# Attention with learned feature maps beside a Mish feed-forward, on one core: key weights moved to ACT's queue, with a new order of all steps

## The chip, the core and the metric

The kernel runs on one core of one Trainium2 chip. The metric is the device time of one execution in microseconds (us). Three runs of the kernel before took 149.74, 149.78 and 149.93 us, so its median is 149.78. The engines are TensorE (PE, with its weight loads PEld), VectorE (DVE), ScalarE (ACT), GpSimd (POOL) and SyncE (SP). ACT and SP also issue the DMAs; each has a queue of its own for them.

## The reference

One block of a model on 2048 tokens of width 448. A layer norm without weights feeds two branches, whose results are added to the input:

```python
xn = _layernorm(x)
# branch A: linear attention, 16 heads of width 28
q, k, v = split(xn @ wqkv)
pq, pk  = q @ w_phi, k @ w_phi                       # per head
phi_q   = concat(softmax(pq), softmax(-pq))          # 56 features per head
phi_k   = concat(softmax(pk), softmax(-pk))
kv, z   = phi_k^T @ v, sum over tokens of phi_k
o       = (phi_q @ kv) / (phi_q @ z + 1e-6)
# branch B
h   = xn @ w1 + b1                                    # 1792 wide
act = h * tanh(softplus(h))                           # Mish
out = x + o @ wo + act @ w2
```

All inputs are bf16.

## The kernel before, in words

**Tiles.** The 2048 tokens are 16 tiles of 128 (`t`), handled in 8 pairs (`u`). The width 448 is three rows of 128 and a rest of 64 rows. So that the array is full, the rest rows of the two tiles of a pair are multiplied at the same time, each in one half of the array's rows. Work for a pair is cut into parts: `E` and `O` are three matmuls over all 128 rows for the even and the odd tile; `A` and `B` are six half-row matmuls each, which run two at a time; `H` is the rest, two half-row matmuls. `E`+`O`+`H` and `A`+`B`+`H` give the same result.

**Weights.** The feature maps are folded into the projections: `W @ w_phi` is made on the core for queries (`Wpq`) and keys (`Wpk`). For the keys the weights are turned on PE in two halves (`w_tr`, L548: eight transposes each, step names `wtk0`, `wtk1`), copied out of PSUM into `Eq0`, multiplied by the block matrix `Wbd` that holds `w_phi` (`w_mm`, L572, steps `wmk0`, `wmk1`), and copied to `Wpk`. The query weights come already turned by the DMA (`lqT0` to `lqT3`, L312), their last 64 columns are doubled by DVE (`qd`, L316), and `wmq0`, `wmq1` multiply them. The first transposes of the keys (half 1) want three loads: `Wkv` rows 0 to 383 of the keys (`lkm`, L303), and the last 64 rows of keys and values twice, once for each half of the array (`lkt`, L308, called tails here). The value weights are `lvm`, L303. The load of `w_phi` (`lp`, L329, four DMAs) must follow the clearing of `Wbd` on POOL (`pwp`, L378).

**Stages.** At the start `x` is loaded in pairs of tiles or four tiles (`lx4.6`: tiles 4 and 5). DVE or ACT take mean and variance (`st`), ACT or POOL the reciprocal root (`rs`, `rp`), DVE or ACT normalize (`xn`), and PE with a copy (`xt..E`, `xt..O`, L514) or a DMA on SP (`xt..m`, L525) turn the result to `xnT`. Then come the projections: `v` (copied by ACT or DVE), `k` and `q` (each followed by two exponentials on ACT, L613 and L679), with the first parts of the feed-forward `f` (Mish on ACT, L698) in between. Key features are normalized by DVE sums and reciprocals (L621, L623) and a product on POOL or DVE (`kn`, L625); query features go through DMA transposes on SP (`e`, L687). `kv` (L643) sums over the tokens, `kvz` brings that sum through a DMA transpose into `KVZ`, `nd` (L721) gives numerators and denominators, DVE divides, `ot` (L758) turns the result, and `wo` (L861) and `gx`, `g` (L842, L827) add both branches into PSUM; DVE adds `x`, and the output is stored.

**What sets the order.** The table `ORDER` names all steps, and `run_order` calls them in that order. Each engine, and each engine's DMA queue, carries out its own part of that list strictly in order; before an instruction stand waits for what it needs from other engines. `s`, `a`, `d`, `p` at the end of a name choose the engine (SP, ACT, DVE, POOL), `b` for `wtk` means both ACT and DVE, each half of the copy. PSUM is eight banks, taken as four pairs: a projection takes the pair that was left longest ago, and PE must wait until the copy or the exponentials that read it have ended.

**The start in this order.** POOL makes zeros, the identity matrix (`pi`) and the other constants. `warm` multiplies zeros (L406), to keep PE busy before data is there. `b1` (L692) turns the bias, between 10 and 4 of these.

```python
def load_main(eng, name, dst, src):                                        # L302
    dma(eng, lambda e: e.dma_start(dst[:, 0:3, :], ...), w=[(name, 0)], tag="ld" + name)
...
r = rows_of("Wk")[:1 + 2 * h] + [("ident",)]                               # L550
```

Of the kernel before, what the change touches and what calls it, by code (L numbers as in the profile page):

```python
# [176 lines left out]


ORDER = """
zero pi ph pp0 table lx6.8a z10 lx4.6s pwp lkms lba st4d lps lkta lx2.4s st5d st6d pe st7a pp1 lvms b1 rp4a z4 xn4d xn5d pp2 rp6a pv xn6d  # L180
lx12.16s lqT3 lqT2 wtk1a xt2Ea xn7d wtk0d lqT1 xt3Ea xt2Oa xt3Od st3d wmk1a st2d wmk0a rp2p st12d lqT0 st15a st14d v2Ba lx8.12s v3Ha v2Ha
v3Aa xn3d v2Aa v3Ba rp14p qd k2H lx0.2s k2E xn2d st13d wmq0d wmq1a k2O xn15a k3E k3O q2B rp12p st8d xn12d q3A xn13d st9d xt1m ep l1ts xn14d
k3H rp8p q2H xn8d xn9d q2A q1B st10d q3B xt6m st11d xt7m st1d q1A st0d xt4m rp10p v1Bd q3H v1Hd v1Ad rp0p k1H xn1d q1H k1O k1E l1ms k6E k6O
k4E xn0d xn11d k4O xt0Ed e6 e7 xt0Od e2 e3 k6H k4H xn10d v4Bd k7A v4Ad kn1.1p v4Hd k7H kn6.0p k0B k7B k0H k0A q6B v7Ba q6H v0Aa v7Aa v7Ha
q6A xt5m v0Ba kn7.0p kn2.1d e5 e4 q4B v0Ha f0.2B q4H q4A f0.3B f0.2A kn3.1p f0.3H f0.3A kn6.1p f0.2H f0.0B kn0.1p kn7.1p v5Bd pk f0.0H f0.0A
kn2.0p v5Ad v5Hd q5A e13 q5H q0A e12 q5B v6Bd l2.2s e8 k5A l2.0a q0H kn0.0p kn4.1p los v6Ad v6Hd kn4.0p q0B kn1.0d k5H f0.12A f0.12H k5B
f1.12B kn5.1d kn5.0p kn3.0d kv6 kv7 kv0 f1.12H f1.12A e9 f1.0A f1.0H f0.12B f1.0B f0.7B kv1 kv4 kv2 f0.8H f0.7A f0.8A f0.7H f0.13H f0.8B
f0.13A f1.8B f0.13B kv5 kv3 e10 f1.8H kvz f1.10B f1.11B f1.10H e11 f1.10A f1.11H f0.10H f1.8A f1.11A f0.1H f0.10A f0.1A f1.3H f0.10B nd5
f1.3A f0.1B f1.7B f1.3B f1.7A f1.7H nd7 q7H q7A f0.6A q7B f1.1A nd6 f0.6H e0 f1.1B f0.6B f0.11B f1.6A f1.1H f1.6H f0.11A f1.6B e15 f0.11H
l2.3a e14 f1.9A f1.2B f0.4B f1.2A f1.2H ot3m nd3 e1 f1.9H f0.4A f1.9B f0.5H f0.4H f0.9B f0.5B nd0 f0.9A f1.13B f0.9H f0.5A f1.5B f1.13H nd2  # L190
f1.13A l2.1s f1.5A f1.4B f1.5H ot1m nd4 f1.4A gx3A nd1 gx2A ot2m wo3A wo3H wob nd11 f1.4H ot0m gx3B wo3B nd13 wo1H gx1A nd12 ot6m wo2A wo2H
gx0A nd9 wo0B wo2B wo1A gx2B gx1B wo1B wo0A nd8 gx6B nd15 gx6A nd10 ot4m sto3 ot5m gx4A nd14 sto1 gx0B gx4B wo6H ot7m wo5H wo0H wo6B gx5B
wo5B wo7H wo4A wo6A wo5A gx5A wo7A wo4B wo7B wo4H g14 g15 sto4 sto2 sto5 sto0 stt14 sto6 stt15
"""


# [809 lines left out]
```

## Time and profile before

| | |
|---|---|
| median of three runs | 149.78 us (149.74 to 149.93) |
| the profiled execution | 149.73 us, of which the span of the instructions is 147.9 |
| PE busy | 143.0 us, 97% of the span, 1844 matmuls |
| DVE, ACT, POOL busy | 106.6, 77.9, 28.9 us |
| chain that ended last | PE 92%, DMA 3%, ACT 2%, ACT's queue 1%, DVE 1% |
| granted TensorE clock | 1.00 |
| DMA | 17.02 MB, 115 GB/s mean |

Times in the views are from the start of the span. A matmul's duration in the views is longer than its share, since matmuls follow one another before the last has ended; what one costs in a row is the distance from start to start. Two half-row matmuls run side by side, so a row of `x28` with half rows is 14 pairs. A wait is put down to what came last; "issue" is time in which nothing is waited for.

### The profile page before, as it was taken

The page shows a single profiled execution, that of the slowest core. Times are in us where ns is not written, and L with a number is a line of the kernel's source. Part 1 is how long each engine was busy: PE and PEld are TensorE (multiplying, and loading weights), DVE is VectorE, ACT ScalarE, POOL GpSimd, SP SyncE. Part 2 cuts the span into 40 slices and gives each one's busy share as a digit, 9 for nine tenths or more (in the row PEclk, how much of TensorE's full clock was granted, in tenths as well). Part 3 has the DMA queues.
Part 4 walks back from the last instruction along what each step waited for, and adds up shares of the span by engine and source line. Part 5 has one row for each costly group of instructions (what it writes and reads, how often), then busy time and mean ns, then how long its engine had stood idle before and what let it go on. Part 6 is the DMA issues. An engine that isn't in the chain of part 4 may idle for free.

```text
span 147.9 us, 4201 instructions
## 1 busy us (share of the span) xinstructions
PE 143.0 (97%) x1844; PEld 76.3 (52%) x1844; DVE 106.6 (72%) x217; ACT 77.9 (53%) x96; POOL 28.9 (20%) x41
## 2 busy tenths in 40 slices
PE   7699999999999999999999999999999999999993
PEld 2275445555555554445444445555555555556652
DVE  0899987999999997217942889979973999433432
ACT  3699999999998966778997583030000000000000
POOL 5005333373999606000000000000000000000000
DMA  5997998998999400090069502220020040600063
GB/s 132 301 243 224 169 184 277 226 160 203 114 329 275 50 4 0 20 194 7 0 146 225 156 4 62 66 62 0 4 64 4 0 124 4 177 14 0 0 241 131
DMA packets 39125, 17.02 MB, mean 115 GB/s; under 512 B 33092, under 2 KB 38340, under 8 KB 39108
## 3 DMA queue, kind: packets, MB, share of 16 engines
q1 hardware_dynamic: 37704, 15.40, 47.4%
q10 hardware_dynamic: 1404, 1.36, 3.1%
q8 instruction: 14, 0.23, 0.7%
q14 instruction: 3, 0.02, 0.1%
HBM read 7.02 MB, written 1.84 MB: 60 GB/s over the span
## 4 chain that ended last, share of the span: by engine, by line
PE 92%; DMA 3%; ACT 2%; ACTq 1%; DVE 1%; issue 0%
PE PS L441 51%; PE PS L842 25%; PE PS L861 7%; PE PS L827 3%; DMA Wkv<-in_A_wqkv_dram 3%; PE PS L721 2%; PE PS L643 2%; ACT xnT L519 1%; ACT Eq L519 1%; PE PS L572 1%; ACTq L337 0%; PE PS L548 0%; DVE x_all L792 0%; ACTq L308 0%; ACT L357 0%; PE PS L514 0%
## 5 line engine op out<-in xcount | busy, mean ns | idle before, releaser
L441 PE MATMUL PS<-xnT,W 64*128 64x512 bf16 x392 | 45.2, 376 | 0.0
L842 PE MATMUL PS<-W,actT 64*128 64x448 bf16 x392 | 39.1, 349 | 0.0
L698 ACT ACTIVATE actT<-PS,b1T 128x1024 bf16<-128x1024 f32 x28 | 29.9, 1113 | 14.5 <-PE PS L441 14.5
L441 PEld LDWEIGHTS PS<-xnT,W 64*128 64x128 bf16 x392 | 18.8, 94 | 20.3 <-ACT actT L698 0.4
L842 PEld LDWEIGHTS PS<-W,actT 64*128 64x128 bf16 x392 | 19.0, 94 | 16.7
L625 POOL TENSOR_TENSOR actT<-actT,rSk 128x896 bf16<-128x896 bf16 x12 | 20.1, 1698 | 12.9 <-DVE rSk L623 12.9
L792 DVE TENSOR_TENSOR x_all<-PS,x_all 128x448 bf16<-128x448 f32 (+1 forms) x16 | 9.3, 616 | 16.0 <-PE PS L861 9.4
L621 DVE TENSOR_REDUCE Sk<-actT 128x32 f32<-128x896 bf16 x16 | 16.8, 1049 | 0.0
L613 ACT ACTIVATE actT<-PS 128x896 bf16<-128x896 f32 x16 | 13.8, 941 | 0.3 <-PE PS L441 0.2
L441 PE MATMUL PS<-Wkv,xnT 64*128 64x448 bf16 x112 | 12.9, 350 | 0.3 <-ACT xnT L519 0.3
L441 PE MATMUL PS<-Wpq,xnT 64*128 64x448 bf16 x112 | 13.0, 349 | 0.0
L441 PE MATMUL PS<-Wpk,xnT 64*128 64x448 bf16 (+1 forms) x82 | 12.6, 351 | 0.0
L480 DVE BATCH_NORM_STATS2 stats<-x_all 128x6 f32<-128x448 bf16 x14 | 8.5, 605 | 4.2 <-DMA x_all<-in_A_x_dram 4.2
L737 DVE COPY Sq<-PS 128x32 f32<-128x32 f32 x16 | 3.0, 186 | 11.8 <-PE PS L721 11.8
L746 DVE TENSOR_TENSOR v_all<-v_all 128x464 f32<-128x464 f32 x16 | 10.3, 642 | 0.6
L742 DVE TENSOR_TENSOR v_all<-PS,Sq 128x464 f32<-128x464 f32 x16 | 10.3, 641 | 0.5
L750 DVE TENSOR_TENSOR xn<-v_all,rden 128x448 bf16<-128x448 f32 x16 | 10.0, 625 | 0.6
L744 DVE TENSOR_TENSOR v_all<-PS,Sq 128x464 f32<-128x464 f32 x16 | 10.1, 629 | 0.0
L679 ACT ACTIVATE actT<-PS 128x896 bf16<-128x896 f32 x10 | 8.8, 946 | 0.0
L441 PEld LDWEIGHTS PS<-Wkv,xnT 64*128 64x128 bf16 x112 | 5.6, 94 | 5.4 <-PE PS L441 0.9
L441 PEld LDWEIGHTS PS<-Wpq,xnT 64*128 64x128 bf16 x112 | 5.7, 94 | 4.7 <-DVE stats L480 0.4
L441 PEld LDWEIGHTS PS<-Wpk,xnT 64*128 64x128 bf16 (+1 forms) x82 | 5.5, 95 | 5.0 <-issue 0.7
(82 smaller groups left out, 133.8 us busy)
## 6 DMA issues: line engine op xcount, KB each, us to landing
out_dram<-x_all SPq DMA_DIRECT2D x7, 224.0 KB, 2.2
W<-in_B_w_dram SPq DMA_DIRECT2D x1, 1344.0 KB, 7.5
x_all<-in_A_x_dram SPq DMA_DIRECT2D x2, 448.0 KB, 4.3
x_all<-in_A_x_dram SPq DMA_DIRECT2D x3, 224.0 KB, 3.7
Wkv<-in_A_wqkv_dram SPq DMA_DIRECT2D x2, 336.0 KB, 4.3
Wo<-in_A_wo_dram SPq DMA_DIRECT2D x2, 336.0 KB, 4.1
W<-in_B_w_dram SPq DMA_DIRECT2D x2, 224.0 KB, 3.8
W<-in_B_w_dram ACTq DMA_DIRECT2D x1, 448.0 KB, 4.1
```

Of the source, the lines that this page charges most:

```text
L441: ins = e.matmul(o, lhs(c, k), rhs(c, k), start=par in first and n == at[par][0], stop=par in last and n == at[par][-1])
L613: op("ACT", lambda e, s=s: e.activation(E_of(u)[:, s, :, :], two(b, D), ACT.Exp, scale=1.0 if s == 0 else -1.0), r=[pb(b), pb(b + 1)], w=[ ...
L621: op("DVE", lambda e: e.tensor_reduce(Sk[u][:, s, :], Eh(), AX.X, ALU.add), r=[("E", u, s)], w=[("Sk", u, s)], tag=f"Sk{u}.{s}")
L625: op(eng, lambda e: e.tensor_tensor(Eh(), Eh(), ap_on(rSk[u][:, s, 0:1], [[1, 2 * H], [0, DH]]), ALU.mult), r=[("E", u, s), ("rSk", u, s)] ...
L698: op("ACT", lambda e: e.activation(actT[:, fc, q * 1024:(q + 1) * 1024], bank(b, 2), ACT.Mish, bias=b1T[:, fc:fc + 1]), r=[("b1T",), pb(b) ...
L742: op("DVE", lambda e: e.tensor_tensor(tv(t1), num(0), sx(1), ALU.mult), r=[pb(b), pb(b + 1), ("Sq", i)], w=[("t1", i)], tag=f"ta{t}")
L744: op("DVE", lambda e: e.tensor_tensor(tv(t2), num(1), sx(0), ALU.mult), r=[pb(b), pb(b + 1), ("Sq", i)], w=[("t2", i)], tag=f"tb{t}")
L746: op("DVE", lambda e: e.tensor_tensor(t1, t1, t2, ALU.add), r=[("t1", i), ("t2", i)], w=[("t1", i)], tag=f"tc{t}")
L750: op("DVE", lambda e: e.tensor_tensor(o_sb[k][:, t % 2, :].rearrange("p (h d) -> p h d", d=DH), t1[:, :, 0:DH], ap_on(rden[i][:, 0:1], [[1 ...
L792: op("DVE", lambda e: e.tensor_tensor(x_all[:, t, 0:n], bank(b)[:, 0:n], x_all[:, t, 0:n], ALU.add), r=[pb(b), ("x", t)], w=[("out", t)], ...
L842: ins = e.matmul(bank(b)[:, 0:D], actT[lo:hi, fc, tok(2 * u + par)], W2[lo:hi, fc, 0:D], start=first and fc == 0, stop=last and fc == FC - 1)
L861: ins = e.matmul(bank(b)[:, 0:w], oT_of(u)[lo:hi, cc * P:(cc + 1) * P], Wo[lo:hi, cc, 0:w], start=first and n == at[par][0], stop=last and ...
```

## The change

Only the table `ORDER` is changed; every step's code is as it was. Its first lines, before and after:

```diff
-zero pi ph pp0 table lx6.8a z10 lx4.6s pwp lkms lba st4d lps lkta lx2.4s st5d st6d pe st7a pp1 lvms b1 rp4a z4 xn4d xn5d pp2 rp6a pv xn6d
+pp2 ph zero lx4.6s pp1 pv pe pp0 st5d lx6.8a lba pwp lps lkta table lkma st4d lx2.4a st7a st6d rp4a pi z10 xn4d rp6a xn5d lvms z4 wtk1b
...
```

The heads of the two DMA queues are the first place. On ACT (`x_all` is the pair of tiles 6 and 7, at the end tiles 2 and 3; `64x896` are the two tails; `128x3x448` the main key weights):

```order
-L357 ACT_TABLE_LOAD
 L300 DMA x_all<-in_A_x_dram 128x896
 L337 DMA b1_rows<-in_B_b1_dram 14x128
 L308 DMA Wkv<-in_A_wqkv_dram 64x896 x2
+L357 ACT_TABLE_LOAD
+L303 DMA Wkv<-in_A_wqkv_dram 128x3x448
+L300 DMA x_all<-in_A_x_dram 128x896
```

The key weights and one pair of `x` come to ACT's queue behind the tails, and the table load stands behind the tails too. On SP (the first `Wkv` row is the key weights, the second the value weights; `128x1792` are four tiles of `x`):

```order
 L300 DMA x_all<-in_A_x_dram 128x896
-L303 DMA Wkv<-in_A_wqkv_dram 128x3x448
 L329 DMA Wbd<-in_A_w_phi_dram 28x4x28 x4
-L300 DMA x_all<-in_A_x_dram 128x896
 L303 DMA Wkv<-in_A_wqkv_dram 128x3x448
 L300 DMA x_all<-in_A_x_dram 128x1792
 L312 DMA_TRANSPOSE WqT<-in_A_wqkv_dram 128x448 x4
 L300 DMA x_all<-in_A_x_dram 128x1792
+L308 DMA W1<-in_B_w1_dram 64x1792 x2
+L525 DMA_TRANSPOSE xnT<-xn1 128x7x128
 L300 DMA x_all<-in_A_x_dram 128x896
```

Those two loads are gone from SP, `w_phi` is second, and behind the query weights the tails of `W1` and the first transpose of `xn` stand ahead of the last pair of `x`.

The second place is PE from its first work on data (`ident,Wkv` are the transposes of the key weights, `ident,xn` those of tokens, `Wbd,Eq` the key products, `Wbd,WqT` the query products, `Wkv,xnT` values, `Wpk,xnT` keys). Before:

```order
L548 MATMUL PS<-ident,Wkv 112x128 x8
L514 MATMUL PS<-ident,xn 128x128 x3
L548 MATMUL PS<-ident,Wkv 112x128 x8
L514 MATMUL PS<-ident,xn 128x128 x11
L572 MATMUL PS<-Wbd,Eq 128x112 x16
L441 MATMUL PS<-Wkv,xnT 128x448 x28
L441 MATMUL PS<-Wpk,xnT 128x448 x5
```

and of the change:

```order
L548 MATMUL PS<-ident,Wkv 112x128 x16
L514 MATMUL PS<-ident,xn 128x128 x10
L572 MATMUL PS<-Wbd,Eq 128x112 x16
L441 MATMUL PS<-Wkv,xnT 128x448 x5
L514 MATMUL PS<-ident,xn 128x128 x4
L441 MATMUL PS<-Wkv,xnT 128x448 x3
L692 MATMUL PS<-ident,b_rows 128x14
L441 MATMUL PS<-Wkv,xnT 128x448 x3
L441 MATMUL PS<-Wpk,xnT 128x448 x6
```

All 16 key transposes stand together, four token transposes and that of the bias moved behind the first value matmuls, and whole-row passes (`E`, `O`: three matmuls) took the place of pairs of half-row ones at the first values.

The third place is ACT's row of copies that feeds this (`Eq0<-PS` are the copies of turned key weights, `xnT` those of turned tokens, `v_all` a pair's values; `junk1` are the statistics of one tile):

```order
+L519 ACTIVATE Eq0<-PS 112x512
 L519 ACTIVATE Eq0<-PS 112x1024
-L519 ACTIVATE xnT<-PS 128x384 x2
+L519 ACTIVATE xnT<-PS 128x384
+L519 ACTIVATE Wpk<-PS 128x896 x2
 L519 ACTIVATE xnT<-PS 128x512
-L519 ACTIVATE Wpk<-PS 128x896 x2
+L519 ACTIVATE v_all<-PS 128x32x28
 L472 ACTIVATE junk1,mv<-x_all 128x448
```

ACT takes one copy of `xnT` fewer and half a copy of key weights more, makes `Wpk` earlier, and copies one pair of values ahead of the statistics; the other pair's copy, which stood with it behind the statistics, now follows the first exponentials. On DVE the other half of the first key copy and two copies of `xnT` take the place of a full key copy and one copy of `xnT`.

Further on, two of the four value copies that ACT had go to DVE, three token normalizations go from DVE to ACT and two pieces of one from ACT to DVE, and two of the four normalizing products of the key features that DVE had go to POOL. The passes of `q`, `k`, `v` and `f` are interleaved anew, the `kv` sums run in two groups of four pairs instead of three groups (3, 3 and 2), the tiles of `nd` come in another order, and the loads of `Wo` move behind the transposes of most query features.

More of the change, by code (lines that the diff above doesn't have):

```diff
@@ L179 @@
 ORDER = """
-zero pi ph pp0 table lx6.8a z10 lx4.6s pwp lkms lba st4d lps lkta lx2.4s st5d st6d pe st7a pp1 lvms b1 rp4a z4 xn4d xn5d pp2 rp6a pv xn6d
-lx12.16s lqT3 lqT2 wtk1a xt2Ea xn7d wtk0d lqT1 xt3Ea xt2Oa xt3Od st3d wmk1a st2d wmk0a rp2p st12d lqT0 st15a st14d v2Ba lx8.12s v3Ha v2Ha
-v3Aa xn3d v2Aa v3Ba rp14p qd k2H lx0.2s k2E xn2d st13d wmq0d wmq1a k2O xn15a k3E k3O q2B rp12p st8d xn12d q3A xn13d st9d xt1m ep l1ts xn14d
-k3H rp8p q2H xn8d xn9d q2A q1B st10d q3B xt6m st11d xt7m st1d q1A st0d xt4m rp10p v1Bd q3H v1Hd v1Ad rp0p k1H xn1d q1H k1O k1E l1ms k6E k6O
@@ L184 @@
[L184 to L191, printed above, removed]
@@ L192 @@
-gx0A nd9 wo0B wo2B wo1A gx2B gx1B wo1B wo0A nd8 gx6B nd15 gx6A nd10 ot4m sto3 ot5m gx4A nd14 sto1 gx0B gx4B wo6H ot7m wo5H wo0H wo6B gx5B
-wo5B wo7H wo4A wo6A wo5A gx5A wo7A wo4B wo7B wo4H g14 g15 sto4 sto2 sto5 sto0 stt14 sto6 stt15
+pp2 ph zero lx4.6s pp1 pv pe pp0 st5d lx6.8a lba pwp lps lkta table lkma st4d lx2.4a st7a st6d rp4a pi z10 xn4d rp6a xn5d lvms z4 wtk1b
+lx12.16s wtk0a xn6d xt2Od lqT0 xt2Ed lqT3 lqT1 xt3Ea xn7d wmk1a st2d lqT2 st3d wmk0a v2Ha st12d rp2p v2Oa xt3Oa v2Ea b1 st13d v3Ea qd k2E
@@ new lines @@
+k2O st15a st14d wmq1a xn3d rp14p lx8.12s xn2d wmq0d l1ts v3Oa rp12p k2H st8d xn14a xn15d xn12d v3Ha st9d k3B q2A k3H rp8p k3A xn13d q2H q3A
+xt1m q2B q3H st10d q1E xn8d lx0.2s q1O v1Bd xt7m q3B xn9d st0d v1Ad st1d k1A xt6m st11d k1H v1Hd q1H rp0p xt4m xn1d l1ms k1B xn0d k6H e6 e7
+k6E k4O k4E xt0Ed rp10p xt0Od k6O k4H v0Hd kn2.1p v4Hd v4Ad v0Ad xn11a e2 kn3.1p v4Bd e3 v0Bd k7H k7A v7Ad v7Hd k7B k0B xn10a kn6.1p q6A
+xt5m kn1.0p k0A k0H kn4.1p q6H e5 q4B v7Bd q6B q4A f0.2B q4H f0.0B kn7.1p kn6.0p e4 f0.2A f0.0H f0.3B ep f0.0A v5Ad f0.2H f0.3H f0.3A v5Bd
@@ new lines @@
+kn2.0p kn1.1p k5A kn7.0p v5Hd v6Hd k5H v6Ad kn3.0p k5B e12 q5B e13 v6Bd kn5.0d kn0.1d pk kn4.0p l2.0s q5H q5A q0B f0.13H q0H q0A kn5.1p
+kn0.0p kv7 kv2 kv6 kv1 f0.12B f0.13B f1.0H f0.12H f0.13A f1.0A f0.12A f1.0B f0.1A f0.1H f1.12A e0 f0.1B f0.7H f1.12B l2.2a f0.7A f1.12H e8
+f0.8B f0.7B f0.8A f0.8H kv3 kv5 kv4 kv0 f0.10A kvz f1.8H f1.8A f1.11H l2.1s f1.11A f1.8B f0.10B f1.11B f1.3A e9 f0.10H f1.7B f1.3H nd4 f1.7A
+f1.7H f1.10B f1.3B f1.10H nd0 f1.10A q7H e1 q7A nd5 q7B f0.6A f0.6H f1.1H l2.3s f1.1A e11 e10 f0.6B f1.1B f0.11B f1.5A f1.5H los f0.11H e14
@@ new lines @@
+f0.11A f1.2B f1.5B f1.9B nd2 f1.2A ot2m f1.2H f1.9A f1.9H nd3 f0.5A f0.5H f0.9B f0.5B f0.4B f0.9A f0.9H e15 f0.4H nd6 f1.4B f0.4A wo2B f1.4A
+f1.4H f1.13B f1.6H wo2A nd7 gx2B f1.13A nd1 gx2A gx3A f1.6A wo2H ot3m ot0m ot1m wo3A f1.6B wo3B nd11 f1.13H gx3B wo1H nd12 gx1A wo1A wo0B
+nd10 wo3H gx0B nd8 gx0A ot5m nd9 wo1B gx1B nd13 gx5B wo0A wo5A nd15 wo5H ot6m gx5A sto2 nd14 sto1 gx6B ot4m ot7m sto3 gx4B wo5B wo6A gx6A
+gx4A wo6H wo4A wo7B wob wo4H wo6B wo7A wo4B wo0H wo7H g14 sto0 sto5 stt14 sto4 g15 sto6 stt15
```

## The prediction

> **What bounds the kernel now.** I read the page's busy times and slices first, then the same in three stretches, then the list of waits, then the chain that ended last.
>
> From the page, the span, busy time by engine, and the slices of ACT:
>
> ```profile
> span 147.9 us, 4201 instructions
> PE 143.0 (97%) x1844; PEld 76.3 (52%) x1844; DVE 106.6 (72%) x217; ACT 77.9 (53%) x96; POOL 28.9 (20%) x41
> ACT  3699999999998966778997583030000000000000
> ```
>
> TensorE carries the kernel; ACT is full beside it from the third slice (7.4 us) to the twelfth (44 us). The view by stretches (length, PE busy, granted clock), with borders at the first matmul on real data, the first projection and the last product:
>
> ```profile
> 7.03:10.05 3.02, 2.73 (x47) 1.00 1.22 302
> 10.05:144.99 134.94, 134.94 (x1772) 1.00 0.49 107
> ```
>
> A busy PE need not be PE at its peak, so the list of waits must confirm it. PE's waits there are two at the warm-up and b1, before 5 us, and these:
>
> ```profile
> PE PS L548 <- DMA Wkv<-in_A_wqkv_dram: 1.0, 1, 1.0
> ...
> PE PS L441 <- ACT xnT L519: 0.3, 1, 0.3
> ```
>
> None lies behind 10.05. The chain in order of time shows what the start waits for, and the pace afterwards:
>
> ```profile
> 2.47 4.52 DMA Wkv<-in_A_wqkv_dram
> ...
> 7.03 0.67 PE PS L548 x8
> ...
> 7.72 1.02 ACT Eq L519
> ...
> 10.05 3.74 PE PS L441 x33
> 13.79 0.83 PE PS L572 x16
> ...
> 25.66 0.39 PE PS L514 x7
> ...
> 59.31 6.58 PE PS L441 x60
> ...
> 90.13 2.65 PE PS L842 x28
> ```
>
> Behind 10.05 the kernel is a row of matmuls without holes: 28 half-row matmuls in 2.65 us are 14 pairs at 0.189 us. The start is a chain: the second key tail is issued at 2.47, lands at 6.99, eight transposes, ACT's copy of them, three copies of xnT, first value matmul. So only three things can move the time: when the key weights are there (call T the first transpose of them, now 7.03), how long it is from T to the first projection (3.02), and new holes behind it. The number of passes is the same before and after, and a whole-row pass of 3 takes the place of 3 pairs.
>
> **The change part by part.** The span is 147.94 in an execution of 149.73; the median shown is 149.78, so one profile stands 0.05 from it. I add to 149.73.
>
> *Queues at the start.* The issues of before in the timeline (start, length):
>
> ```profile
> 0.75 1.28 ACT L357 ACT_TABLE_LOAD   x1 [0.75 <-PEq L991]
> ...
> 0.78 0.39 ACTq L300 DMA_DIRECT2D x_all<-in_A_x_dram  x1
> ...
> 1.20 0.41 SPq L303 DMA_DIRECT2D Wkv<-in_A_wqkv_dram  x1
> ...
> 1.92 1.16 ACTq L308 DMA_DIRECT2D Wkv<-in_A_wqkv_dram  x2
> ...
> 1.99 1.82 SPq L329 DMA_DIRECT2D Wbd<-in_A_w_phi_dram  x4
> ...
> 2.21 0.53 POOL L381 MEMSET v_all<- 128x256 uint32 x1
> ...
> 4.27 0.43 SPq L303 DMA_DIRECT2D Wkv<-in_A_wqkv_dram  x1
> ```
>
> The main key weights were issued second on SP, at 1.20. Now they stand on ACT behind a pair of x, b1, both tails and the table load. The loads ahead keep their issue times and end at 3.08 (1.92 + 1.16). The table load takes ACT 1.28, but a load was issued 0.03 behind its start, so it holds up no issue, and the key weights go out at about 3.1, 1.9 us later, and become the last of the three pieces that the transposes want. Time from issue to landing is not shown for this place; the nearest rows are those of the same lines (smallest, median, largest):
>
> ```profile
> L303 SPq DMA_DIRECT2D Wkv<-in_A_wqkv_dram x2: 415/425/435, 1.2 to 4.3; - x2
> ...
> DMA to landing us min/median/max: 4.0/4.6/7.5
> ...
> DMA to landing us min/median/max: 3.4/3.7/5.0
> ```
>
> The two 336 KB loads took 4.0 and 4.6; the 7.5 is W1's 1344 KB. In the second row, that of the loads of x on L300, the quickest took 3.4. So the landing is at 6.5 to 7.7. I take 3.8, just under the value weights' 4.0: that load stood behind another one in its ring as the key weights do now, but SP's ring is emptier here, with w_phi alone in it until about 3.9. That gives 6.9 and T = 6.94: **-0.09**.
>
> The Trainium skill bears on this, in "DMA: Bandwidth & Descriptors", section "Queues, rings and completion order": ACT and SP own one ring each on the same 16 engines, which take turns between rings. By that rule a change of ring gives no bandwidth; what is wanted first (two pairs of x, b1, key weights, tails) is the same set of bytes, so T would stay at 7.03 and the sum be 0.09 higher. The trace agrees as far as it goes: beside the median of 3.7 for loads of x, mostly SP's, ACT's own has this row (section 6 of the page):
>
> ```profile
> x_all<-in_A_x_dram ACTq DMA_DIRECT2D x1, 224.0 KB, 3.6
> ```
>
> *w_phi second on SP.* It waits for the clearing of Wbd on POOL, now eighth in its row instead of sixth. All of POOL's preparations ended at 2.74 (2.21 + 0.53), so in any order w_phi goes out between 1.99 and 2.74; I take 2.1. Queued behind that wait on SP are the value weights, the query transposes and the rest of x. The four issues last 1.82, so the value weights go out near 3.95 (at most 4.6) instead of 4.27, since two other loads left SP's row. By 4.0 to 4.6 more they land at 8.0 to 9.2, and are wanted at T + 2.9: 9.8. Cost 0; were w_phi late by x beyond T + 1.7, where the key products start, x would be paid in full. The identity, now POOL's last, is there by about 2.7, long before T. The x pair at the end of ACT's row, issued at 3.5, is wanted by DVE at about 9.5: 6 us for a load of 3.4 to 5.0.
>
> *From T to the first projection.* Here ACT's row decides. Its timeline of before:
>
> ```profile
> 8.64 1.35 ACT L519 ACTIVATE xnT<-PS 128x384 bf16<-128x384 bf16 x3
> ...
> 9.86 1.75 ACT L519 ACTIVATE Wpk<-PS 128x896 bf16<-128x896 f32 x2
> ...
> 11.46 0.62 ACT L472 ACTIVATE junk<-x_all 128x448 bf16<-128x448 bf16 x1
> ...
> 13.10 1.70 ACT L519 ACTIVATE v_all<-PS 128x896 bf16<-128x896 f32 x2
> ...
> 14.69 0.98 ACT L519 ACTIVATE Wpq<-PS 128x448 bf16<-128x448 f32 x2
> ...
> 15.54 1.74 ACT L613 ACTIVATE actT<-PS 128x896 bf16<-128x896 f32 x2
> ...
> 17.14 1.07 ACT L504 ACTIVATE xn<-x_all,shift,rstd 128x64 bf16<-128x64 bf16 x2
> ```
>
> From start to start: the 1024-wide copy 0.92 (7.72 to 8.64), a copy of xnT 0.41, both Wpk 1.60, statistics of one tile 1.64, a v copy 0.80, both Wpq 0.85, both exponentials 1.60. In the new order ACT copies half of the first transposes (DVE the other half), then all of the second. The first half copy starts at T + 0.69 as now and takes about 0.48 (estimate: half of 0.92 and a start), the 1024-wide one runs T + 1.17 to T + 2.2, eight key products at 0.05 (0.83 for 16) follow, and v2H starts at T + 2.65 instead of T + 3.02: **-0.37**. DVE's copies of xnT end at about T + 2.1 and hide. But four transposes of tile 7 (0.056 each, from the 0.39 for seven) and b1's, which stood in the idle time before T, now lie behind: 0.22 + 0.11 = **+0.33**. Together nearly nothing.
>
> *New holes behind it.* k3B takes banks that Wpq's copies must leave. ACT's row until then: 0.48 + 0.92 + 0.41 + 1.60 + 0.45 + 0.80 + 1.64 + 0.85, from T + 0.69, with the last copy's end T + 7.95. PE gets there with 21 slots of 0.189, 16 products at 0.05, four transposes and b1: 5.10 behind T + 2.65, so T + 7.75. **+0.20**. Then v1B wants banks of the exponentials of k3: ACT T + 7.85 + 1.60 + a normalization 0.65 (estimate: two pieces took 1.07 to their end) + v3's copy 0.80 + 1.60 and its end 0.15, so T + 12.6; PE is there 24 slots later, T + 12.5. **+0.10**. Bounds: 0, if ACT's steps run 4% quicker than I add, to 0.8, if both waits and two like them later (f0.0B on DVE's v7, v0H on exk1, each with under 0.1 of margin in the same adding) all open by 0.2.
>
> *Work between engines.* Two of four v copies go from ACT to DVE, two of four normalizations of phi_k from DVE to POOL:
>
> ```profile
> L625 POOL TENSOR_TENSOR actT<-actT,rSk 128x896 bf16<-128x896 bf16 x12 | 20.1, 1698 | 12.9 <-DVE rSk L623 12.9
> ...
> L625 DVE TENSOR_TENSOR actT<-actT,rSk 128x896 bf16<-128x896 bf16 x4 | 6.1, 1522 | 0.1
> ...
> L521 DVE CAST v_all<-PS 128x896 bf16<-128x896 f32 x4 | 4.3, 1068 | 0.3 <-PE PS L441 0.3
> ```
>
> DVE gives 3.0 and takes 2.1; POOL takes 3.4, of 12.9 that it idles. Adding DVE's row up from its last xnT copy near 26 (16 sums with reciprocals at 1.35, five v copies at 1.03, two normalizations at 1.5, small ones 0.5) ends at 56.3, POOL's last product at 58.7, wanted by kv0 at about 59.3: hidden by 0.6; past that every 0.1 is paid. ACT's row changes between the tables of Exp and Mish as often as before. KVZ follows the last kv product by 28 pairs instead of 30 (60 matmuls in 6.58, from 59.31): 6.1 us. Its transpose is issued and lands so:
>
> ```profile
> 61.40 1.24 SPq L667 DMA_TRANSPOSE KVZ<-KVT  x1
> ```
>
> with 3.2 to landing on the page, so 61.40 + 3.2 - 59.31 = 5.3 are used and 0.8 is left: nothing to pay.
>
> **Sum:** -0.09 - 0.37 + 0.33 + 0.20 + 0.10 = +0.17, so 149.73 + 0.17 = **149.9**. About 0.2%, or 0.3 us, is what a measurement of this kernel can tell from no change: I forecast none.
>
> **Rivals.** *Key weights late (slower).* If their load takes the 4.6 that the same load took, T is 7.74, and all behind moves: +0.71 instead of -0.09, 150.7. For it: it is issued 1.9 us later and behind four loads. Against: it took 4.6 with the x pairs ahead in full flow; by 3.1 they are nearly in. It decides from a landing of 4.0 on (then 150.1). Chance 0.17.
>
> *Banks, not bytes (slower).* T as forecast, but the waits on ACT and DVE come out at the upper bound 0.8 instead of 0.3: 150.4. For: ACT is full until 44, and the new row has a v copy and a normalization between k2 and k3. Against: that row is no longer as a whole: what it takes in there has left it before the first projection. Chance 0.16.
>
> *Early weights, no holes (faster).* Landing after 3.4: T = 6.54, -0.49; with -0.37 + 0.33 and no new wait it is -0.53, 149.2. For: both tails no longer share the rings with the main weights. Against: 336 KB have nowhere taken under 4.0. Chance 0.21.
>
> *A cold array (slower).* The first zero matmuls run at half pace:
>
> ```profile
> 0.89 3.63 PE L406 MATMUL PS<-zeros 128*128 128x512 bf16 x10 [0.89 <-POOL zeros L363]
> ...
> 4.96 1.05 PE L406 MATMUL PS<-zeros 128*128 128x512 bf16 x4
> ```
>
> Ten took 3.63, the last four 1.05. Now all 14 stand together, start 0.17 later and end at 5.3 to 5.7, so PE is idle for 1.2 to 1.6 us before T instead of 1.0. If it fell back, the 42 small matmuls before v2H (2.3 us) would take twice as long, about half of it under ACT's chain: +1, 150.9. The Trainium skill ("TensorE: Matmul & The Clock Gate", table in "Part 1: The HAM clock gate") puts the fall at an idle window of about 3.4 us; by that rule nothing is lost. The trace agrees for 1.0 us and shows no longer gap. Chance 0.03.
>
> **How the numbers follow.** Forecast 0.43, late weights 0.17, banks 0.16, cold 0.03, early 0.21. Faster by over 0.2% is 0.21, within it 0.43, slower 0.36. The range goes from 149.3 (a little inside the faster case) to 150.6 (most of both slower ones).
>
> **What would show it.** Key weights issued on ACT near 3.1 and landing near 6.9; the first transpose of them right behind; first value matmul 2.65 after that; a hole of PE near 15 before k3B with ACT's Wpq as its releaser, and none above 0.1 later; PE without idle from 20 on, and 2.95 from its last product to the span's end (147.94 - 144.99). It is wrong if the wait at the start ends on something else than this load (w_phi, identity, DVE's x), if PE waits for POOL or DVE near 46 or 59, or if the stretch from the first projection to the end of PE grows by more than 0.8.

## The result

The changed kernel is slower by 1.1%. Six runs took 150.88 to 151.62 us, median 151.38; six of the kernel before on the same chip 149.74 to 149.93, median 149.76. The ratio is 1.0108, with a 95% interval of 1.0092 to 1.0124. Forecast was 149.9, range 149.3 to 150.6: the time lies above it.

The profiled execution took 151.55, of which the span is 149.35. Its page, the lines that the prediction shows of before:

```profile
span 149.3 us, 4191 instructions
PE 144.6 (97%) x1838; PEld 74.3 (50%) x1838; DVE 103.9 (70%) x218; ACT 77.9 (52%) x96; POOL 31.5 (21%) x43
ACT  1888899979999986767998671005000000000000
```

The shares read as before: nothing here says that time was lost. The stretches do (length, then PE, PEld, DVE, ACT, POOL busy, granted clock, DMA share, GB/s), with borders at T, the first projection and PE's last product:

```profile
7.29:10.08 2.79, 2.73 (x43) 2.29 (x44) 1.98 (x7) 2.07 (x4) 0.00 (x0) 1.00 1.39 305
10.08:146.39 136.31, 135.59 (x1773) 69.67 (x1771) 98.28 (x201) 72.13 (x83) 29.62 (x29) 1.00 0.49 106
```

The span grew by 1.41: T by 0.26 (7.03 to 7.29), T to the first projection by -0.23 (3.02 to 2.79), the row of matmuls behind it by 1.37 (134.94 to 136.31). PE is busy in 135.59 of those 136.31, where it was busy in all of 134.94: 0.65 is new work in this stretch or slower pace, 0.72 is idle. The list of PE's waits (us in total, times, longest) names that idle time, and DVE's list what stands behind it:

```profile
PE PS L572 <- DVE WqT L316: 0.7, 1, 0.7
PE PS L548 <- DMA Wkv<-in_A_wqkv_dram: 0.4, 1, 0.4
```

```profile
DVE stats L480 <- DMA x_all<-in_A_x_dram: 5.3, 2, 4.0
```

Before, DVE waited for x once, at the start, and the pair of tiles 2 and 3 went out on SP (it landed at 7.55, 3.70 later):

```profile
DVE stats L480 <- DMA x_all<-in_A_x_dram: 4.2, 1, 4.2
...
3.85 0.38 SPq L300 DMA_DIRECT2D x_all<-in_A_x_dram  x1
```

In the changed kernel the query products (L572) wait for DVE's doubling of the query weights, and DVE itself had waited twice for x: 4.0 at the start and 1.29 later. The chain that ended last shows which load:

```profile
3.76 7.35 DMA x_all<-in_A_x_dram
11.11 0.02 issue
11.13 0.64 DVE stats L480
...
13.50 0.54 DVE stats L480
...
14.25 0.24 DVE WqT L316
14.48 0.05 issue
14.53 0.96 PE PS L572 x16
...
17.12 9.76 PE PS L441 x83
```

It is the pair of tiles 2 and 3, last on ACT's queue: issued at 3.76, landed at 11.11, 7.35 later. Four statistics and the bias copy stand behind it on DVE, then the doubling, so the products start at 14.53 instead of about 13.66, a hole of 0.87 in PE's row (matmul starts 1060 ns apart, where 190 is the pace). A second one of 0.17 follows at 17.1, before the queries that need DVE's Wpq. From 17.12 PE runs without a wait. The issues of the two queues, from the timeline:

```profile
3.12 1.28 ACT L357 ACT_TABLE_LOAD   x1 [3.12 <-issue]
3.15 0.57 ACTq L303 DMA_DIRECT2D Wkv<-in_A_wqkv_dram  x1
3.76 0.50 ACTq L300 DMA_DIRECT2D x_all<-in_A_x_dram  x1
```

The key weights went out at 3.15 and landed at 7.20, 4.05 later.

So the theory was that the heads of the queues cost all of it, in two ways: by T and by the late pair of x. The rivals were that the new order of the other steps costs it, or only the place of the doubling in DVE's row.

### The profile page after: what moved, and what is told of

It reads as the page before. It is cut to its first block, busy times and chain, and to the rows that moved or that the text cites. A ratio compares the mean times of both kernels' runs of the same rounds, so it can differ in the third digit from the quotient of the medians.

```text
span 149.3 us, 4191 instructions
## 1 busy us (share of the span) xinstructions
PE 144.6 (97%) x1838; PEld 74.3 (50%) x1838; DVE 103.9 (70%) x218; ACT 77.9 (52%) x96; POOL 31.5 (21%) x43
## 4 chain that ended last, share of the span: by engine, by line
PE 88%; DMA 5%; DVE 3%; ACTq 1%; ACT 0%; issue 0%; DVEq 0%
PE PS L441 48%; PE PS L842 25%; PE PS L861 7%; DMA x_all<-in_A_x_dram 5%; PE PS L827 3%; PE PS L721 2%; PE PS L643 2%; DVE stats L480 1%; ACTq L308 1%; PE PS L572 1%; ACTq L337 0%; ACT L357 0%; DVE x_all L792 0%; DVE mv L481 0%; ACTq L300 0%
## 5 line engine op out<-in xcount | busy, mean ns | idle before, releaser
L625 POOL TENSOR_TENSOR actT<-actT,rSk 128x896 bf16<-128x896 bf16 x14 | 23.3, 1700 | 10.8 <-DVE rSk L623 6.5
L441 PE MATMUL PS<-Wkv,xnT 64*128 64x448 bf16 (+1 forms) x100 | 13.3, 350 | 0.0
L441 PE MATMUL PS<-Wpq,xnT 64*128 64x448 bf16 (+1 forms) x106 | 12.8, 350 | 0.0
L441 PEld LDWEIGHTS PS<-Wpq,xnT 64*128 64x128 bf16 (+1 forms) x106 | 5.1, 94 | 5.4 <-DVE Wpq L521 0.5
L441 PEld LDWEIGHTS PS<-Wkv,xnT 64*128 64x128 bf16 (+1 forms) x100 | 5.1, 94 | 4.8 <-ACT actT L613 0.5
```

The source lines that it names most:

```text
L441: ins = e.matmul(o, lhs(c, k), rhs(c, k), start=par in first and n == at[par][0], stop=par in last and n == at[par][-1])
L625: op(eng, lambda e: e.tensor_tensor(Eh(), Eh(), ap_on(rSk[u][:, s, 0:1], [[1, 2 * H], [0, DH]]), ALU.mult), r=[("E", u, s), ("rSk", u, s)] ...
```

## Experiments

All are edits of the table `ORDER`; the diffs show only the steps that were moved and their neighbours of the same kind, in their order. One execution of each was profiled. "V" is the start of the first projection; the last column is V to PE's last product. The time of before is that of the same chip.

| | time (before) | T | V - T | behind V |
|---|---|---|---|---|
| before | 149.76 | 7.03 | 3.02 | 134.94 |
| after | 151.38 (149.76) | 7.29 | 2.79 | 136.31 |
| e1 x2 on SP | 151.05 (149.62) | 7.62 | 2.79 | 135.37 |
| e2 doubling earlier | 151.12 (149.62) | 7.08 | 2.79 | 136.39 |
| e3 new order, old heads | 149.62 (149.62) | 6.65 | 2.79 | 135.40 |
| e4 old order, new heads | 150.76 (149.62) | 7.77 | 3.02 | 135.12 |
| e5 key weights on SP | 150.12 (149.60) | 6.56 | 2.79 | 135.46 |
| e6 tiles 12 to 15 later | 151.83 (149.60) | 7.20 | 2.79 | 136.71 |
| e7 key weights early on ACT | 150.41 (149.60) | 7.38 | 2.79 | 135.37 |
| e8 tails first | 151.85 (149.60) | 7.81 | 3.44 | 135.15 |
| e9 key weights on ACT, x6 on SP | 150.85 (149.70) | 6.73 | 3.35 | 135.37 |
| e10 the same, 10 zero matmuls | 152.02 (149.70) | 6.67 | 3.67 | 135.37 |
| e11 e3 with the bias early | 149.58 (149.70) | 6.53 | 2.82 | 135.94 |
| e12 x2 ahead of key weights | 154.68 (149.73) | 10.36 | 3.53 | 135.73 |

In this table and below, "x2" is the pair of tiles 2 and 3, "x6" that of 6 and 7, "x12" the four tiles from 12.

One trace tells T to some tenths only. With the same heads of before it was 7.03, 6.65 (e3) and 6.53 (e11), and with the same heads of the change 7.29, 7.08 (e2) and 7.77 (e4).

### Heads or order: e3 and e4

e3 has the order of the change with the heads of before (DMA steps of both queues and the table load back in their old places, the last pair of x and the tails of `W1` further on too):

```diff
-lx4.6s lx6.8a lba lps lkta table lkma lx2.4a lvms
+table lx4.6s lx6.8a lba lkms lps lkta lx2.4s lvms
```

> The new order of all steps with the queue heads of before: key weights second on SP, then w_phi, both pairs of x and the value weights behind them; table load first on ACT; x of tiles 0 and 1 and the tails of W1 as before. Late x or late keys: the transposes of the key weights start at 7.0 instead of 7.29, the first value matmul at about 9.8, no hole before the query products: 149.9 to 150.1, about the kernel before. Rival (the new order itself): a hole over 0.5 stays: 150.8 or more.

Measured: ratio 1.0002 (0.9985 to 1.0019), 0.3 below the expected range, since T was 6.65 and not 7.0. PE's waits and the stretches:

```profile
PE PS L548 <- DMA Wkv<-in_A_wqkv_dram: 0.5, 1, 0.5
```

```profile
6.65:9.44 2.79, 2.73 (x43) 2.29 (x44) 2.59 (x10) 2.23 (x5) 0.00 (x0) 1.00 1.51 315
9.44:144.84 135.40, 135.34 (x1773) 71.61 (x1772) 98.04 (x201) 71.96 (x83) 29.72 (x29) 1.00 0.50 106
```

Beside that for the zeros of the warm-up this is PE's only wait, and PE is busy in 135.34 of 135.40. The new order alone gives V - T -0.23 and behind it +0.46, of which 0.33 are the transposes and the bias that moved. The rest is before v1B, at 19.3, where two starts are 409 ns apart; in the changed kernel, which does not wait there, they are 285 apart.

e4 is the other half, the heads of the change in the order of before:

```diff
-table lx6.8a lx4.6s lkms lba lps lkta lx2.4s lvms
+lx6.8a lx4.6s lba lps lkta table lkma lx2.4a lvms
```

> The order of before with the queue heads of the change. Late x: the pair of tiles 2 and 3 lands near 11, and in the old row DVE wants it at 9.3 with five pieces of statistics and normalization ahead of the doubling, so the query products move from 13.6 to about 14.6; key transposes at 7.3: 150.9 to 151.3. Rival (the new order itself is to blame, the heads are not): only the 0.26 of the later key weights, 150.0.

Measured: ratio 1.0074 (1.0053 to 1.0096). Its chain:

```profile
3.15 4.58 DMA Wkv<-in_A_wqkv_dram
7.73 0.04 issue
7.77 0.67 PE PS L548 x8
```

The key weights took 4.58, T is 0.74 later, and behind V 0.18 is lost (135.12 to 134.94). The late pair that was expected near 11 did not come: x2 landed at 9.03, and no step of PE waited for it. So the heads are the cause in either order, but here by T alone.

### The hole at the query products: e1 and e2

e1 puts x2 back on SP, where it stood, between w_phi and the value weights:

```diff
-lkma st4d lx2.4a
+lkma st4d lx2.4s
```

> The changed kernel with one load moved: the pair of x of tiles 2 and 3 goes back to SP's queue, between w_phi and the value weights. Theory (late x): in the changed kernel this pair landed 7.35 us after its issue, at 11.11, DVE's statistics waited for it, and with them the doubling of the query weights (14.25) and PE (hole of 0.87 before the query products at 14.53). Expected then: the pair lands by 8.7, the statistics of tile 2 start before 10, the doubling before 13.3, no hole of PE over 0.2 there, and about 1.0 us less than the changed kernel: 150.3. Rival (the new order itself): the doubling stands too late in DVE's row whatever lands; the hole stays over 0.6 and the time at 151.2.

Measured: ratio 1.0096 (1.0068 to 1.0123). x2 landed at 8.08 and the hole is gone (behind V 0.94 less than the changed kernel). But the key weights took 4.38, with as much ahead of them as in the changed kernel, and T is 0.33 later; so the time can't be told from that of the changed kernel (1.0108), and the forecast of 150.3 missed. What the hole alone costs in time, e7 below shows.

e2 leaves the heads of the change and lets DVE double the query weights ahead of the bias copy and of the statistics of tile 13:

```diff
-b1 st13d v3Ea qd
+qd b1 st13d v3Ea
```

> The changed kernel with one DVE step moved: the doubling of the query weights stands ahead of the bias copy and the statistics of tile 13. All loads as changed. Late x: the pair still lands near 11, but the doubling is done at about 13.4 instead of 14.48, so PE's hole shrinks from 0.87 to 0.1 or less; DVE is still late for its Wpq copies, so 0.2 to 0.4 stays before the first query pass: 150.6. Rival (order alone): about the same number, but with the pair's wait still 1.3 on DVE it can't go under 150.4; if it does, the late pair costs nothing by itself. Second rival (the turned query weights land late, at 12.97): the hole stays over 0.5.

Measured: ratio 1.0096 (1.0069 to 1.0124): no gain that can be told, where 150.6 was expected. The hole shrank from 0.87 to 0.14, and another one opened at 16.99, as PE's waits show:

```profile
PE PS L441 <- DVE Wpq L521: 0.8, 1, 0.8
```

The statistics that x2 had held up only changed places with the doubling; the next thing that PE wants of DVE, Wpq, stood behind them. In this row of DVE the late load is paid once, wherever the step that shows it is put. T was set by the key weights here too: they landed at 6.99, 0.09 before T, as in the changed kernel (7.20 and 7.29).

### Late issue or place in the ring: e5, e7, e12

e5 gives the key weights alone back to SP (second, issued at 1.20); x2 stays last on ACT:

```diff
-lx4.6s lx6.8a lba lps lkta table lkma lx2.4a
+lx4.6s lkms lx6.8a lba lps lkta table lx2.4a
```

> Only the key weights go back to their place on SP (second, ahead of w_phi); the pair of tiles 2 and 3 stays last on ACT's queue. Theory A, the rings are shared by turns and a load waits for what stands ahead of it in its own ring: the key weights land near 5.5, T is set by the tails again (6.5 to 7.1), and the pair of x, with nothing but the tails ahead of it on ACT's ring, lands by 8.5, so DVE does not wait for it and no hole stands at the query products: 149.7 (149.5 to 149.9). Theory B, the end of ACT's ring is slow whatever stands ahead in it, since SP's ring is full of large loads: the pair lands at 10.5 or later, the hole at the query products is 0.5 or more, 150.3 to 150.6.

Measured: ratio 1.0042 (1.0015 to 1.0069), with runs from 149.57 to 151.40; the profiled one took 149.85. T 6.56, x2 landed at 7.14, no hole at the query products. Theory A's numbers held in the profiled execution. The median is 0.2 above its range; why some runs are a us longer isn't known, since one was traced, but it isn't the clock (0.998 to 1.000 in all ten).

e7 keeps the key weights on ACT, but second there, issued at 1.19:

```diff
-lx6.8a lba lps lkta table lkma lx2.4a
+lx6.8a lkma lba lps lkta table lx2.4a
```

> The heads of the change, but on ACT the key weights stand second, ahead of b1, tails and table load, and are issued near 1.2 as before the change. Theory A: T is set by when all three pieces are through ACT's one ring, whatever their order, since the same bytes stand in that ring: the key weights land at about 5.7, the tails behind them at 6.8 to 7.3, T is 6.9 to 7.4, the pair of x lands near 11 and the hole at the query products stays: 151.0 to 151.5. Rival, the late issue (3.15 instead of 1.2) is what costs: T is 6.5 or less, and without an idle ring at 3.5 to 4.5 the pair lands by 10: 150.4 or less.

Measured: ratio 1.0056 (1.0033 to 1.0079). Both sides were half right. T is 7.38, as theory A had it: the key weights landed at 5.44, but now the tails are last, and late:

```profile
2.99 4.30 DMA Wkv<-in_A_wqkv_dram
7.29 0.09 issue
7.38 0.64 PE PS L548 x8
...
8.12 0.42 DVE Eq L521
8.54 0.32 DVE xn L508
...
8.91 0.34 PE PS L514 x3
9.25 0.99 PE PS L572 x16
```

But x2 landed at 8.20 instead of 11.11, in the same place with the same loads ahead, and the hole is gone. So in that place x2 is late when the key weights go out late. As T is that of the changed kernel within 0.1, the two ratios also show in time what the hole costs: 1.0108 less 1.0056, some 0.8 us, and their intervals do not meet. The stretch from 3.5 to 4.5 (last column GB/s) shows what that did, first before, then the changed kernel, then e7:

```profile
3.50:4.50 1.00, 1.00 (x5) 0.28 (x3) 0.30 (x1) 0.09 (x1) 0.00 (x0) 1.00 1.11 377
```

```profile
3.50:4.50 1.00, 1.00 (x4) 0.34 (x3) 0.49 (x1) 0.99 (x2) 0.00 (x0) 1.00 0.71 124
```

```profile
3.50:4.50 1.00, 1.00 (x4) 0.34 (x3) 0.51 (x1) 0.86 (x1) 0.00 (x0) 1.00 1.08 367
```

With the key weights issued at 3.15, little was in the queues at 3.5 but w_phi and the tails, so about 250 KB (377 less 124 GB/s for 1 us) was not moved then: more than a pair of x. All that stood behind was moved later, when the value weights, x12 and the query weights were on their way too.

The gap alone does not make the later loads late. e1, whose key weights also go out at 3.15, has it as well:

```profile
3.50:4.50 1.00, 1.00 (x4) 0.34 (x3) 0.51 (x1) 0.99 (x2) 0.00 (x0) 1.00 0.51 102
```

Yet there the value weights landed at 8.95, x12 at 10.13 and the last query weights at 12.08, as early as in e7 (9.06, 10.23, 12.03), against 9.98, 11.48 and 12.96 in the changed kernel. It takes the gap and a pair of x at the end of ACT's queue together; how the two work on each other, no run here takes apart.

e12 exchanges the last two loads of the change's head:

```diff
-table lkma st4d lx2.4a
+table lx2.4a lkma st4d
```

> The changed kernel with the last two loads of ACT's head exchanged: the pair of tiles 2 and 3 ahead of the key weights, both issued between 3.1 and 4.4. Theory A (a load waits for what stands ahead of it in its ring, and the end of a ring that shares with the value weights and tiles 12 to 15 is slow): the pair lands at 6.8 to 7.5 and the hole at the query products (0.87) goes, but the key weights take its place and land at 7.8 to 8.6, T is 7.9 to 8.7 instead of 7.29: 150.9 to 151.7, no gain. Rival, the key weights cost nothing there and only the pair's place at the end was wrong: T stays within 0.3 of 7.29, 150.4 to 150.6.

Measured: ratio 1.0324 (1.0258 to 1.0390), far more than either side had. x2 landed at 6.65, 3.5 after its issue; the key weights, now last, took what x2 had taken:

```profile
3.76 6.51 DMA Wkv<-in_A_wqkv_dram
10.27 0.09 issue
10.36 1.07 PE PS L548 x16
11.43 1.03 PE PS L514 x10
12.47 1.49 PE PS L572 x16
```

So with both loads behind the tails the last place is slow, whichever load stands there: 7.35 for 224 KB in the changed kernel, 6.51 for 336 KB here. The last row shows a second cost: 16 products of a kind that took 0.83 before take 1.49. PE had been idle for 4.40 us ahead of T, and about 1 us after it had started again the granted clock was 0.50 for 3.41 us (third number from the right):

```profile
11.34:14.75 3.41, 3.41 (x32) 2.63 (x30) 3.30 (x11) 3.15 (x5) 0.14 (x1) 0.50 1.20 311
```

The page of the Trainium skill that the prediction used for the cold array ("TensorE: Matmul & The Clock Gate", "Part 1: The HAM clock gate") lets the array fall back after an idle window of about 3.4 us. This agrees; in e10's trace, with 1.15 idle before T and 0.87 behind the key transposes, the clock stayed at 1.00 and the same 16 took 0.82.

### What x2 shares the end with: e6

x12 goes behind the query weights on SP, and its statistics behind the doubling on DVE:

```diff
-lx12.16s lqT0 lqT3 lqT1 lqT2 st12d b1 st13d qd
+lqT0 lqT3 lqT1 lqT2 lx12.16s b1 qd st12d st13d
```

> The heads of the change, but on SP the four tiles 12 to 15 of x are loaded behind the query weights, and their statistics on DVE follow the doubling of the query weights. Theory A (rings by turns): the 448 KB of that load no longer take turns with ACT's ring while the pair of tiles 2 and 3 is on its way, so the pair lands at 8.5 to 9.7 instead of 11.1, and the query weights at 11 to 11.5 instead of 13; the hole at the query products (0.87) goes, 150.3 to 150.6. Theory B (the end of ACT's ring is slow in itself): the pair still lands near 11, DVE still waits for it, 151.2 or more.

Measured: ratio 1.0143 (1.0126 to 1.0160). x2 landed at 9.57 instead of 11.11, and the query weights at 11.33 instead of 12.97, as theory A had it: the load on the other queue had held x2 up. The time is worse, and not 150.3 to 150.6, because DVE now waits for x12 and PE for DVE (DVE's timeline, then PE's wait):

```profile
13.22 0.63 DVE L480 BATCH_NORM_STATS2 stats<-x_all 128x6 f32<-128x448 bf16 x1 [0.77 <-DMA x_all<-in_A_x_dram]
...
16.22 1.15 DVE L521 CAST Wpq<-PS 128x448 bf16<-128x448 f32 x2
```

```profile
PE PS L441 <- DVE Wpq L521: 0.8, 1, 0.8
```

### What sets T: e9 and e10

e9 is e7 with x6 moved from ACT's queue to the second place on SP:

```diff
-lx4.6s lx6.8a lkma lba lps lkta table lx2.4a
+lx4.6s lx6.8s lkma lba lps lkta table lx2.4a
```

> The heads of the change, but ACT's queue begins with the key weights (then b1, tails, table load and the pair of tiles 2 and 3), and the pair of tiles 6 and 7 stands second on SP. So the key weights stay on ACT's ring, with 560 KB in it up to the last tail instead of 784 KB. Theory A (T is set by what stands in one ring up to the last piece wanted, since the two rings take turns): the key weights land near 5, the tails near 6.0 to 6.6, and T is 6.3 to 6.9 instead of 7.1 to 7.4; the pair of tiles 2 and 3 lands by 8 and no hole of more than 0.3 stands behind the first projection: 149.3 to 149.8. Rival, key weights on ACT are late in themselves: T stays at 7.1 to 7.4, 150.3 to 150.7.

Measured: ratio 1.0083 (1.0067 to 1.0099). T is 6.73: the key weights on ACT are not late in themselves, T follows how much stands in one queue ahead of the last key piece. The forecast of the time missed, because x6 was now late (it landed at 5.22 instead of 4.16), and its statistics on ACT and normalization held the first projection:

```profile
1.19 4.03 DMA x_all<-in_A_x_dram
...
7.71 0.58 DVE xn L508 x2
```

Over all runs with the tails and key weights in one queue behind x6 (784 KB), T was 7.29, 7.62, 7.08, 7.77, 7.20 and 7.38. In those where a queue held at most 560 KB up to the last key piece (before, e3, e5, e9, e10, e11) it was 7.03, 6.65, 6.56, 6.73, 6.67 and 6.53. The two groups do not meet. (e8 and e12 are left out: in e8 the bias set T, and in e12 the key weights stood behind x2.)

e10 takes four of the 14 zero matmuls out of e9:

```diff
-z10 xn4d rp6a xn5d lvms z4
+z8 xn4d rp6a xn5d lvms z2
```

> The same with 10 instead of 14 of the zero matmuls ahead of the first data (the output is not touched by them). Where these are slow up to their end, 14 take PE until 6.2 to 6.9, and so hold T back; 10 end 0.9 to 1.7 earlier. Theory A: T equals the landing of the last tail plus 0.1, so if the tails land at 6.0 to 6.6 this gives 0 to 0.3 over the kernel with 14: 149.2 to 149.7. Rival, the array stays slow for longer with fewer of them: the 32 key products and transposes behind T take more than their 0.05 each, first projection more than 2.9 behind T, 150.0 or more.

Measured: ratio 1.0143 (1.0110 to 1.0176), and T 6.67 as with 14. V - T is 3.67 instead of 3.35 in the profiled execution (150.71), by a later x6 (5.48) and PE's wait for its normalization. The other three runs took 151.87 to 152.19. They were not traced, but their clock is on record: 0.989 on the mean, where the traced run and all of e9 have 1.00. The trace of e12 has the same mean, with its 3.41 us at half clock. So with four zero matmuls fewer the clock fell in three runs of four, and these are 1.2 to 1.5 us longer than the fourth. Behind which idle time it fell, only a trace of one of them could show. Theory A's 149.2 to 149.7 missed.

### Two attempts at a faster kernel: e8 and e11

e8 is e3 with the tails ahead of x6 on ACT and the bias turned in the idle time:

```diff
-table lx4.6s lx6.8a lba lkms lps lkta
+table lx4.6s lkta lx6.8a lba lkms lps
```

> The order of the change with the heads of before, and two edits: the two key tails stand ahead of the pair of tiles 6 and 7 on ACT's queue, and the bias is turned in the idle time before T. Theory A: with the heads of before T hangs on the tails, which land at 6.4 to 7.0; issued 1 us earlier and with no load ahead of them they land by 4.6, and T becomes that of the key weights, 5.3 to 5.9 instead of 6.65 to 7.03; the pair of tiles 6 and 7 lands about 1 us later, still in time for its transposes: 148.7 to 149.1. Rival: what is won at T is lost again to tiles 6 and 7 or to the value weights (T plus 2.65 is then ahead of their landing at 8.3 to 9.3), 149.4 to 149.7.

Measured: ratio 1.0166 (1.0125 to 1.0208); both sides missed. The tails landed at 5.77, the key weights at 5.36, but PE waited 1.3 for the rows of the bias, whose load now stood last, with zero matmuls behind it, so T was 7.81; and x6 landed at 6.32, which made the first projection late once more (the longest of the four runs, 152.79, had a clock of 0.988 besides):

```profile
PE PS L692 <- DMA b_rows<-in_B_b_dram: 1.3, 1, 1.3
```

```profile
2.02 4.30 DMA x_all<-in_A_x_dram
...
8.49 0.89 DVE xn L508 x3
```

e11 is e3 with only the bias moved:

```diff
-z10 xn4d rp6a xn5d lvms z4
+z10 xn4d rp6a xn5d lvms b1 z4
```

> The order of the change with the queue heads of before, and the bias turned on PE between the 10 and the 4 zero matmuls as before the change. The stretch from the first projection to the end of PE loses the 0.11 that this costs there: 135.8 instead of 135.9, and the time is 149.5 against 149.6 of the kernel before, if T is the same as with the heads of before (6.65 to 7.03). Rival: PE waits at that place for the load of b1 and the zero matmuls behind it end later than the tails land, T 7.1 or more, 149.9 or more.

Measured: 149.58 against 149.70, ratio 0.9996 (0.9985 to 1.0007): no difference. The profiled execution was its longest (150.19), with a wait that the others need not have, for query weights that landed late:

```profile
PE PS L572 <- DVE WqT L316: 0.5, 1, 0.5
```

No kernel here beats the one before by more than the measurement can tell.

## Why the prediction was wrong

The step that failed is one sentence on the heads of the queues: "The x pair at the end of ACT's row, issued at 3.5, is wanted by DVE at about 9.5: 6 us for a load of 3.4 to 5.0", costed at nothing. The need was rightly placed, near 9.8 (DVE was idle for 1.29 before 11.13), but the load took 7.35. The 3.4 to 5.0 came from loads in queues that had been fed without a break; this one stood behind 336 KB issued after a gap, while three large loads ran on the other queue. It cost 0.87 + 0.17 = 1.04 of the 1.41; e1, e5 and e7 lose the hole when x2 lands by 8.2, and in e2 a move on DVE only put it elsewhere. None of the four rivals named it. The prediction's own sign of being wrong came true: the stretch behind the first projection grew by 1.37, more than 0.8, and the hole hung on DVE's doubling, not on ACT's Wpq.

Point by point:

- **Key weights, -0.09.** Issue near 3.1 was right (3.15). Landing after 3.8 was quick: 4.05 here, 3.83 and 3.95 in e2 and e6, but 4.58 and 4.38 in e4 and e1. Between the two traces the term is +0.26, and between the means of three traces with the same heads, 6.74 and 7.38, +0.64. That is in the direction of the rival "key weights late", whose threshold of 4.0 was just passed; its full price (T 7.74) came only in e4. The reason given, a ring on which little stands, looked at SP's ring; by the two groups of T above what counted was ACT's own, with 784 KB instead of 448.
- **"The same set of bytes".** By the prediction's reading of the Trainium skill's rule on rings ("DMA: Bandwidth & Descriptors", "Queues, rings and completion order"), T would have stayed at 7.03. T did not stay: by the two groups of T above, 784 KB in one queue and 224 KB and w_phi in the other is not the same as 448 and 560, and the stretch from 3.5 to 4.5 (124 for 377 GB/s) was a time in which there was too little to take turns with.
- **T to first projection, -0.37.** Measured -0.23 in the changed kernel, and the same in e1 to e3 and e5 to e7, where x6 was in time too (-0.20 in e11). ACT's row was taken to decide; in e7's chain above, from 8.12 on, it is DVE's copy of the turned keys, its normalization of tile 7, the last three transposes and then all 16 key products, where eight were counted.
- **Work moved behind it, +0.33.** It holds: e3's stretch is 0.46 longer with 0.06 idle.
- **k3B on ACT's Wpq, +0.20; v1B on the exponentials of k3, +0.10.** The changed kernel, e1 and e3 have no such wait before k3B; e6 alone shows one for ACT's Wpq (0.3). Before v1B the distance is 409 ns in e3, e1 and e7 and 285 in the changed kernel: 0.12 where no late pair holds up what comes before. Together 0.1 for 0.30, and nothing in the changed kernel itself.
- **w_phi, table load, work between engines, POOL's products, KVZ: 0.** Right: no wait of PE for POOL or DVE behind 17.12, w_phi was issued at 2.00, and from PE's last product to the span's end it is 2.96 (149.35 - 146.39). For the value weights behind w_phi it was luck: they took 6.13, not 4.0 to 4.6, and landed at 9.98, 0.4 before the first value pass that wants them (10.37).
- **Cold array.** The zero matmuls stayed slow for longer than read from one trace: 14 took 5.80 until 6.87, so PE was idle for 0.4 before T, and not 1.2 to 1.6. The clock was 0.999 or 1.00 in all six runs of the changed kernel, so this rival did not come there; it came in e12 and in three of e10's runs.

Of the 1.82 between the two profiled executions (151.55 and 149.73) 0.41 lies outside the span. Runs of both kernels have 1.8 to 2.3 there, so that part need not be the change's: the medians are 1.6 apart.

What stays open: why the last packets of the load at the end lag so far. In the trace's packet records half of x2's packets had ended at 7.55 and the last at 10.32 (in e7 at 6.60 and 7.88). Which DMA engine carried which packet is not in these records. No run moves the four query transposes of SP's queue either, so their share in it is not known. x2's landing with the same heads was 11.11, 10.81 (e2) and 9.03 (e4).

## What to carry to other kernels

Whoever moves a load to another queue should price every load that stands behind it on both queues, not only the one that is moved: here the moved load lost 0.26, and the one behind it 1.04. Early issue can be worth something to the loads behind: with the key weights issued 2 us earlier (e7), the pair behind them landed 2.9 us earlier. And a late load into an engine that works in order was not cured by the one reordering tried of what that engine does next (e2).

## What was not expected of the hardware

- The last load at the head of ACT's queue took 5.3 to 7.4 us from issue to landing where two large loads were issued behind the tails (the changed kernel, e2, e4, e6, e12), and 3.8 to 4.5 where it was one (e1, e5, e7, e9, e10). In e12 the load just ahead of it, issued 0.6 earlier, took 3.5. SP's value weights were slow with it: 6.13 in the changed kernel, 4.04 before.
- A load can land long after its last packet: in e7 the first tail's last packet ended at 5.15, its landing was seen at 6.93; 0.3 to 0.6 is usual in the same trace for the loads of x. The Trainium skill ("DMA: Bandwidth & Descriptors", "Queues, rings and completion order") says that the write which counts a load up lands only after every earlier write of that DMA engine, from whichever queue; this delay fits that, but no run here took it apart.
- The slow phase of the first matmuls differs between executions: 14 zero matmuls took 5.80 in the changed kernel, 5.11 in e3, 4.89 in e12, all from 1.07. Where they are long, their end comes close to T: in e2 they ended at 6.88, and the key weights that set T landed at 6.99.
